# Issuing a memory-bound kernel's first load ahead of the barrier that opens the program

## The chip, the cores and the metric

The kernel runs on one core of one Trainium2 chip. The time is microseconds of device time; most executions of a kernel agree within about 0.1%. Each execution also lists its span, the time from the program's own first instruction to its last; the span is 1.8 us shorter than the time in nearly every execution. Because the effect in question is near 0.2%, most comparisons below were timed in five rounds, with the kernel before timed on the same chip in the same rounds.

The names: SyncE issues loads, TensorE (PE in the profile) multiplies, VectorE (DVE) and ScalarE (ACT) work on rows of elements, and GpSimd (POOL) fills small tiles. A semaphore is a counter that one engine raises and another waits for. A large load is cut into packets, which the core's 16 DMA engines move.

## The reference, cut to what matters

One decode step for one token: an attention block over a long cache, and an MLP with a mixer, both fed by one layer norm and added to the input.

```python
xn = layernorm(A_x)                                   # one row of 1024
q = (xn @ A_wq)                                       # 1024 x 4096: 32 heads of 128
scores = einsum(q, k_cache) * 128 ** -0.5             # 4 kv heads, 65536 keys, 128 wide
o = einsum(softmax(scores), v_cache)
out = x + o @ A_wo + mixer_mlp(xn, B_w1, B_w2, B_w3, B_w4)
```

Every weight and both caches are bf16 and are read exactly once. There are 170 MB of them, and one token's worth of arithmetic, so the work is mostly a read of memory.

## The kernel before

SyncE issues all the large loads, in one fixed order, into three buffers of 8 MB. A load is issued as soon as a buffer comes free. The first three entries (wq, w3, and w1 with w2) find empty buffers and wait for nothing.

```python
stream = ["wq", "w3", "w12"]
for u in range(NU):                       # NU = 8
    ...                                   # ("K", u), ("V", u); "wo" before the last V
stream.append("w4")

class Stream:
    def pump(self):
        while self.next < len(stream) and self.held < SLOTS:     # SLOTS = 3
            ...
            self.load(it)
    def done(self, it):                   # called when the last reader of a buffer is emitted
        self.tiles.pop(it)
        self.held -= 1
        self.pump()
    def load(self, it):
        t = big.tile([P, ROW], BF16, name="big")                 # 128 x 32768
        go = nc.sync.dma_start
        if it == "wq":
            go(out=t[:], in_=A_wq.rearrange("(p c) n -> p (c n)", c=DC))
        elif it == "w3":
            go(out=t[:, 0:DC * F], in_=B_w3.rearrange("(p c) f -> p (c f)", c=DC))
        ...

x_row = ogpool.tile([32, D], BF16, name="x_row", tag="og")
nc.vector.memset(x_row[:], 0.0)
nc.scalar.dma_start(out=x_row[0:1, :], in_=A_x[0, 0:1, :])       # x, on ScalarE's queue
st.pump()
```

The program opens with a barrier that is not in this source; the framework puts it there. Each engine announces itself (a drain that raises a semaphore), GpSimd collects the four announcements behind four small memsets of its own, and then releases everybody. Only then does SyncE branch to the body and issue the load of wq.

The program ends in order: the last piece of w4 lands, two matmuls add it to the output row, ScalarE casts the row, a small DMA writes it, and a closing barrier follows.

## Time and profile before

| What | Kernel before | Read from |
|---|---|---|
| time | 402.86 us median (402.81 to 403.03, 4 runs) | times |
| span of the profiled execution | 400.9 us | the page's head |
| data moved by the loads' queue | 169.87 MB, 98.4% of sixteen engines' span | the page's queue list |
| issue of the first load | 0.73 us | timeline of SyncE |
| first data packet | 1.73 us | packet records |
| last data packet ends | 396.86 us | packet records |
| from there to the end | 4.04 us | difference |

First the page's slice rows for the DMA engines: the span in 40 equal slices, the mean busy share of the 16 engines in tenths, and the GB/s that they moved. Below are the loads' queue and the bytes.

```profile
DMA  9989999999999999999999999999999999999895
GB/s 412 425 366 433 451 425 425 503 425 418 414 419 432 418 497 420 425 418 425 432 433 471 425 425 418 433 432 432 464 420 425 418 445 394 428 481 432 380 418 205
...
q1 hardware_dynamic: 4560, 169.87, 98.4%
```

There is no slice in which the engines rest, apart from the last few. From its first packet to its last the stream takes 395.13 us, so it runs at 430 GB/s. The Trainium skill's page "DMA: Bandwidth & Descriptors", section Specifications, gives a fabric ceiling of 435 GB/s. The median 64 KB packet takes 2.42 us. Nothing but fewer bytes or an earlier start can therefore take much off this kernel.

Second, the start. These are SyncE's DMA issues in the timeline (start in us, duration in us, what), and the line of SyncE's own waits for the opening barrier (total, times, longest).

```profile
0.73 0.37 SPq L128 DMA_DIRECT2D big<-in_A_wq_dram  x1
1.16 0.42 SPq L130 DMA_DIRECT2D big<-in_B_w_dram  x1
1.63 0.42 SPq L132 DMA_DIRECT2D big<-in_B_w_dram  x1
2.10 0.52 SPq L133 DMA_DIRECT2D big<-in_B_w_dram  x1
```

```profile
SPq L459 <- PEq L459: 0.7, 1, 0.7
```

SyncE waits 0.7 us at the barrier. In the trace's instruction records it announces itself at 0.00 us, as the first of all engines, and is released at 0.65 us. The view puts the wait down to TensorE's queue (PEq), but TensorE had announced itself by 0.32 us; GpSimd's drain, which ends at 0.49 us, is the last thing that the barrier waits for.

Third, the first pieces of the chain of work that ended last, in order of time (start, length, what), and its last load.

```profile
0.67 0.07 issue
0.73 22.05 DMA big<-in_A_wq_dram
22.83 5.89 PE psq L245 x62
28.73 41.32 DMA big<-in_A_k_cache_dram
...
379.92 17.40 DMA big<-in_B_w_dram
```

And what follows the last packet, from the timeline of ScalarE: the cast and the issue of the output write.

```profile
397.78 0.58 ACT L443 CAST out_t<-psB 64x512 bf16<-64x512 f32 x1 [29.53 <-PE psB L179]
398.39 0.58 ACTq L444 DMA_DIRECT2D out_dram<-out_t  x1
```

The chain reads as if the matmuls on wq (psq) set the time of the next load. They release a buffer at 28.73 us, but the load issued then lands 41.32 us later, and 8 MB need only 19.3 us of the stream (by the packet records, from the first packet of one cache load to the first of the next). The rest of the time it stands in the queue behind loads issued earlier: its own first packet starts at 48.4 us. The chain follows what released an issue; it does not show that the issue came long before its data could flow.

### The profile page before, as it was taken

The numbers are of one execution on the slowest core, as the hardware profiler recorded it, in microseconds if no ns is written. First come the engines' busy times: TensorE is split into PE (matmuls) and PEld (weight loads), VectorE is DVE, ScalarE is ACT, GpSimd is POOL, SyncE is SP. The second block draws the span as 40 slices with busy tenths as digits, with TensorE's granted clock in tenths as the row PEclk, the third lists the DMA queues.
The fourth block names the chain that finished last, engine by engine and source line by source line (L and its number), as shares of the span: only waits on it lengthen the run. The fifth ranks groups of instructions, "written<-read, shape, count | busy, mean of one in ns | idle before, by whom it ended". The sixth has DMA issues, their size and how long they took to land.

```text
span 400.9 us, 2563 instructions
## 1 busy us (share of the span) xinstructions
PE 230.4 (57%) x1348; PEld 44.2 (11%) x854; DVE 209.0 (52%) x154; ACT 27.3 (7%) x35; POOL 5.3 (1%) x28
## 2 busy tenths in 40 slices
PE   0470970591668246922965195629453936594985
PEld 0210000010200110010102010201020002000231
DVE  0511010974196549644953894269349931975040
ACT  1001010003000200020002000100100020002000
POOL 2000000000000000000000000000000000000000
PEclk9995795597679666968796799568866986697999
DMA  9989999999999999999999999999999999999895
GB/s 412 425 366 433 451 425 425 503 425 418 414 419 432 418 497 420 425 418 425 432 433 471 425 425 418 433 432 432 464 420 425 418 445 394 428 481 432 380 418 205
DMA packets 4575, 170.01 MB, mean 424 GB/s; under 512 B 467, under 2 KB 469, under 8 KB 982
## 3 DMA queue, kind: packets, MB, share of 16 engines
q1 hardware_dynamic: 4560, 169.87, 98.4%
q8 instruction: 8, 0.13, 0.1%
q14 instruction: 1, 0.01, 0.0%
q10 hardware_dynamic: 6, 0.00, 0.0%
HBM read 169.87 MB, written 0.00 MB: 424 GB/s over the span
## 4 chain that ended last, share of the span: by engine, by line
DMA 52%; DVE 26%; PE 16%; ACT 3%; another core or an unknown queue 2%; issue 1%; DVEq 0%; ACTq 0%
DMA big<-in_A_k_cache_dram 31%; DVE big L315 19%; DMA big<-in_A_v_cache_dram 10%; PE sc L320 8%; PE oacc L370 6%; DMA big<-in_A_wq_dram 6%; DMA big<-in_B_w_dram 4%; DVE p_sb L341 3%; DVE mx L325 3%; ACT p_sb L338 3%; PE psq L245 1%; PE pm_mx L327 0%; DVE m L329 0%; PE pm_mx L334 0%
## 5 line engine op out<-in xcount | busy, mean ns | idle before, releaser
L320 PE MATMUL sc<-big,qdiag 128*128 128x512 bf16 x512 | 127.7, 409 | 66.4 <-DVE big L315 66.4
L315 DVE STREAM_TRANSPOSE big<-big 128x4096 f32<-128x4096 f32 x32 | 139.4, 4413 | 50.5 <-DMA big<-in_A_k_cache_dram 50.4
L370 PE MATMUL oacc<-big,p_sb 128*32 128x512 bf16 x512 | 44.7, 521 | 34.5 <-DVE p_sb L341 34.5
L325 DVE TENSOR_REDUCE mx<-sc 128x1 f32<-128x2048 f32 x8 | 18.3, 2292 | 29.8 <-PE sc L320 29.8
L320 PEld LDWEIGHTS <-qdiag 128*128 128x128 bf16 x128 | 13.0, 102 | 176.6 <-issue 145.9
L338 ACT ACTIVATE p_sb<-sc,nball 128x2048 bf16<-128x2048 f32 x8 | 15.7, 1967 | 218.7 <-DVE nball L336 218.7
L341 DVE STREAM_TRANSPOSE p_sb<-p_sb 128x2048 bf16<-128x2048 bf16 x8 | 18.5, 2311 | 18.0 <-ACT p_sb L338 18.0
L370 PEld LDWEIGHTS <-p_sb 128*32 128x32 bf16 x512 | 16.6, 126 | 59.4 <-DVE p_sb L341 35.1
L245 PE MATMUL psh<-big,ln_rep_b 128*32 128x512 bf16 (+1 forms) x64 | 12.4, 941 | 8.0 <-DMA big<-in_B_w_dram 8.0
L409 PE MATMUL o_acc<-big,oT 128*1 128x512 bf16 x48 | 12.5, 428 | 2.4 <-ACT p_sb L338 2.4
L327 PE MATMUL pm_mx<-ident_f,mx 128*1 128x128 f32 x8 | 2.3, 283 | 19.1 <-DVE mx L325 19.1
L284 DVE STREAM_TRANSPOSE h_row<-h_row 128x896 bf16<-128x896 bf16 x1 | 1.1, 1111 | 21.1 <-ACT h_row L283 21.1
L379 DVE SCALAR_TENSOR_TENSOR og<-oacc,wb,og 128x512 f32<-128x512 f32 x4 | 3.0, 745 | 15.7 <-PE oacc L370 15.7
L179 PE MATMUL psB<-big,hT 128*1 128x512 bf16 x56 | 7.4, 378 | 1.8 <-DMA big<-in_B_w_dram 1.7
L193 PE MATMUL pm_ln<-ln_rowsum_a,ones_f 128*128 128x1 f32 x2 | 0.6, 347 | 13.3 <-DVE ln_rowsum_a L191 13.3
L415 DVE COPY o_rows<-o_acc 1x1024 f32<-1x1024 f32 x1 | 1.2, 1212 | 13.3 <-PE oacc L370 13.3
L184 DVE STREAM_TRANSPOSE x_t<-x_row 32x256 bf16<-32x256 bf16 x4 | 2.5, 616 | 8.9 <-DMA x_row<-in_A_x_dram 8.9
L269 POOL COPY qdiag<-qx 32x32 bf16<-32x32 bf16 x16 | 3.2, 203 | 279.9 <-PE sc L320 249.7
L391 PE MATMUL pm_e<-ol,sel8big 128*128 128x129 f32 x8 | 2.3, 370 | 8.2 <-DVE ol L390 8.2
L245 PE MATMUL psq<-big,ln_rep_a 128*32 128x512 bf16 x64 | 5.9, 547 | 1.3 <-DMA big<-in_A_wq_dram 1.3
L257 DVE CAST q_row<-psq 128x512 bf16<-128x512 f32 x1 | 0.7, 691 | 7.9 <-PE psq L245 7.9
L334 PE MATMUL pm_mx<-ident_f,rep 1*128 1x1 f32 x8 | 1.9, 241 | 5.0 <-DVE rep L331 5.0
(95 smaller groups left out, 72.6 us busy)
## 6 DMA issues: line engine op xcount, KB each, us to landing
big<-in_A_wo_dram SPq DMA_DIRECT2D x1, 8192.0 KB, 36.7
big<-in_B_w_dram SPq DMA_DIRECT2D x1, 7168.0 KB, 38.5
big<-in_B_w_dram SPq DMA_DIRECT2D x2, 2048.0 KB, 46.4
big<-in_B_w_dram SPq DMA_DIRECT2D x2, 1536.0 KB, 27.3
big<-in_B_w_dram SPq DMA_DIRECT2D x1, 1280.0 KB, 24.1
big<-in_B_w_dram SPq DMA_DIRECT2D x1, 1024.0 KB
big<-in_B_w_dram SPq DMA_DIRECT2D x1, 768.0 KB, 30.8
big<-in_B_w_dram SPq DMA_DIRECT2D x1, 512.0 KB, 31.5
```

Source lines behind the costliest of these rows:

```text
L179: nc.tensor.matmul(psB[32 * j:32 * j + lhsT.shape[1], :], lhsT=lhsT, rhs=rhs, start=start, stop=False, tile_position=(0, 32 * j), skip_gro ...
L184: nc.vector.transpose(out=x_t[32 * a:32 * a + 32].rearrange("p c j -> p (c j)"), in_=x_row[:, 256 * a:256 * (a + 1)].rearrange("p (i c) -> ...
L245: nc.tensor.matmul(acc[32 * q:32 * q + 32, i, 0:n], lhsT=rep[:, c, :], rhs=cols(c, i, q), start=(c == 0), stop=(c == DC - 1), tile_positio ...
L269: nc.gpsimd.tensor_copy(out=qdiag[at, LEAD:].rearrange("p (x c) -> p x c", x=4)[:, :, 32 * a:32 * a + 8], in_=qx[at, :, 8 * g:8 * g + 8])
L315: nc.vector.transpose(out=words, in_=words)
L320: nc.tensor.matmul(sc[:, e, :], lhsT=qdiag[:, c0:c0 + P], rhs=cols[:, s, e, :, b2, :, r], start=(s == 0 and b2 == 0 and r == 0), stop=(s = ...
L325: nc.vector.reduce_max(out=mx[:], in_=sc[:].rearrange("p e n -> p (e n)"), axis=AX.X)
L338: nc.scalar.activation(out=p_sb[:], in_=sc[:], func=ACTF.Exp, bias=nball[:, b:b + 1], scale=SCALE, accum_out=group["lall"][:, b:b + 1])
L341: nc.vector.transpose(out=flat, in_=flat)
L370: nc.tensor.matmul(oacc[32 * q:32 * (q + 1), :], lhsT=pT[:, e, 32 * t:32 * (t + 1)], rhs=vt[:, :, e, t, :], start=(e == 0 and t < 4), stop ...
L379: nc.vector.scalar_tensor_tensor(out=og[:], in0=oacc[:], scalar=wb[:, 1:2], in1=og[:], op0=ALU.mult, op1=ALU.add)
L409: nc.tensor.matmul(tail["rows"][0:1, h2, :], lhsT=oT[g][:, j:j + 1], rhs=wt[:, g, j, 512 * h2:512 * (h2 + 1)], start=(g == 0 and j == 0), ...
```

## The change

The first load needs nothing from the barrier: its buffer is untouched and its source is an input. A hook that runs when the program is finished moves that one instruction from the head of SyncE's body to the head of SyncE's entry block, ahead of its announcement at the barrier. No instruction is added or removed.

```diff
+def lead_with_the_first_load(nc):
+    blocks = [block for function in nc.m.functions for block in function.blocks]
+    entry = blocks[0]
+    body = next(b for b in blocks if any(i.opcode == "DMACopy" for i in b.instructions))
+    load = next(i for i in body.instructions if i.engine == mybir.EngineType.SP)
+    assert body is not entry and load.opcode == "DMACopy" and not load.sync_info.on_wait
+    body.instructions = [i for i in body.instructions if i is not load and i.name != load.name]
+    at = next(n for n, i in enumerate(entry.instructions) if i.engine == mybir.EngineType.SP)
+    entry.instructions = entry.instructions[:at] + [load] + entry.instructions[at:]
...
     nc.at_finalize(keep_loaded_weights)
+    nc.at_finalize(lead_with_the_first_load)
```

## The prediction

> What bounds the kernel now. The page's slice rows show the DMA engines at nine tenths or more almost throughout, and the queue list gives the loads' queue 98.4% of sixteen engines' span, for 169.87 MB. Its first data packet starts 1.73 us into the 400.9 us span and its last ends at 396.87 us (packet records): a stream of 395.1 us at 430 GB/s. The Trainium skill's page "DMA: Bandwidth & Descriptors", section Specifications, gives a fabric ceiling of 435 GB/s; the trace agrees: sixteen 64 KB packets at 2.42 us each are 434 GB/s. Idle engine time inside the stream sums to only 1.5 us, half of it in the last slices. So the time is the start, 395.1 us of stream, about 4 us of tail (last matmuls, cast, output write, closing barrier) and about 2 us outside the span (402.85 against 400.9).
>
> What the change does. In the timeline of the first microseconds, SyncE reaches the opening barrier first, at 0.00 us, waits for the others (0.7 us in the queue's own waits), and issues the 8 MB load of wq at 0.735 us; the issue takes 0.37 us and the first packet follows its start by 1.0 us. The change puts this issue ahead of the barrier, at 0.00 to 0.05 us. Nothing is added or removed. SyncE then arrives at the barrier at about 0.42 us (estimate: 0.37 plus an instruction's gap). [...] The three weight loads behind wq should be issued at about 0.73, 1.2 and 1.7 us instead of 1.16, 1.63 and 2.10.
>
> How much is on the critical path. The loads form one stream that never runs dry, so its start moves all of it. wq's landing (22.8 us) moves to about 22.1. Its consumers are ready: the first layer norm's result is done at 16.3 us, although x arrives only at 10.2 us, behind wq's first packets. x may come one packet round (2.4 us) later; 6 us of slack cover it. Later loads are issued as buffers come free, which follows landings and moves with them, each some 15 us before its data flow. So nearly the full 0.7 us should reach the end: first packet near 1.0 us, last end near 396.15, span near 400.2 us, a gain of 0.17%.
>
> Predicted time: 402.15 us, range 401.8 to 402.7. Faster by over 2%: 0.005; within 2%: 0.99; slower by over 2%: 0.005.
>
> What would show the steps right: wq's issue near 0.0 us; the barrier still opening at 0.65 us; wq's landing, later load issues and the last weight piece all about 0.7 us earlier; the stream still 395.1 us long; an unchanged tail.
>
> What would make it wrong: a slower first issue, or SyncE's drain waiting for the load, would open the barrier later, though only the first load's start counts; DMA rings not ready that early would leave nothing; a SyncE that starts later than now would hide the gain; a different interleaving of packets could move the stream by some tenths either way.

## The result, and the profile after

The changed kernel takes 402.10 us (402.02 to 402.14, 4 runs) against 402.86 us, and its output is correct. The ratio is 0.9982, with a 95% interval of 0.9968 to 0.9996. The gain of 0.76 us is small, but no execution of the one kernel overlaps with one of the other. Ratios here and below are not quite the ratio of the medians quoted.

The lines of the changed kernel that answer to those above (line numbers are 12 higher, since the hook was added): slices and queue, SyncE's issues, its wait for the barrier, the chain, and what follows the last packet.

```profile
DMA  9998999999999999999999999999999999999895
GB/s 419 419 453 371 435 471 458 426 419 419 421 426 465 452 426 414 426 426 432 445 460 426 419 426 419 447 439 452 426 421 426 432 445 385 432 481 426 385 417 201
...
q1 hardware_dynamic: 4560, 169.87, 98.6%
```

```profile
0.00 0.38 SPq L140 DMA_DIRECT2D big<-in_A_wq_dram  x1
0.78 0.33 SPq L142 DMA_DIRECT2D big<-in_B_w_dram  x1
1.16 0.42 SPq L144 DMA_DIRECT2D big<-in_B_w_dram  x1
1.64 0.52 SPq L145 DMA_DIRECT2D big<-in_B_w_dram  x1
```

```profile
SPq L471 <- PEq L471: 0.2, 1, 0.2
```

```profile
0.00 22.19 DMA big<-in_A_wq_dram
22.23 6.23 PE psq L257 x59
28.48 40.98 DMA big<-in_A_k_cache_dram
...
379.33 17.39 DMA big<-in_B_w_dram
```

```profile
397.19 0.58 ACT L455 CAST out_t<-psB 64x512 bf16<-64x512 f32 x1 [29.56 <-PE psB L191]
397.80 0.59 ACTq L456 DMA_DIRECT2D out_dram<-out_t  x1
```

The load of wq starts at 0.00 us, and the wait at the barrier shrinks from 0.7 to 0.2 us because SyncE now arrives later. In this trace the last load, the cast and the output write come 0.59 us earlier, and the tail keeps its length. Taken apart by the packet records, the two profiled executions compare like this:

| Part | before, us | after, us | difference |
|---|---|---|---|
| span's start to first data packet | 1.729 | 1.007 | -0.722 |
| stream, first packet to last | 395.134 | 395.270 | +0.136 |
| last packet to end of span | 4.043 | 4.048 | +0.005 |
| span | 400.906 | 400.325 | -0.581 |

The spans differ by 0.58 us and the times by 0.76 us. That is no loss, only the choice of the execution: over the 27 timed executions of the kernel before in the three sets of rounds below, the span is 400.9 to 401.3 us, mostly 401.0 or 401.1, so the profiled one is among its fastest, and the medians of the spans (401.0 and 400.3 us) differ by 0.7 us like the times. The ten profiled executions that move the same bytes on the loads' queue have streams of 395.13 to 395.45 us, and the shortest of them is that of the kernel before. The stretch of 0.14 us is inside that spread.

### The profile page after: what moved, and what is told of

Same layout as the page of the kernel before. It is cut to its first block, busy times and chain, and to the rows that moved or that the text cites. A ratio compares the mean times of both kernels' runs of the same rounds, so it can differ in the third digit from the quotient of the medians. Undisturbed runs are those within 1.5% of the kernel's fastest.

```text
span 400.3 us, 2563 instructions
## 1 busy us (share of the span) xinstructions
PE 236.0 (59%) x1348; PEld 45.2 (11%) x854; DVE 208.9 (52%) x154; ACT 27.3 (7%) x35; POOL 5.3 (1%) x28
## 4 chain that ended last, share of the span: by engine, by line
DMA 51%; DVE 26%; PE 16%; ACT 3%; another core or an unknown queue 2%; issue 1%; DVEq 0%; ACTq 0%
DMA big<-in_A_k_cache_dram 31%; DVE big L327 19%; DMA big<-in_A_v_cache_dram 10%; PE sc L332 8%; PE oacc L382 6%; DMA big<-in_A_wq_dram 6%; DMA big<-in_B_w_dram 4%; DVE p_sb L353 3%; DVE mx L337 3%; ACT p_sb L350 3%; PE psq L257 2%; DVE m L341 0%; PE pm_mx L339 0%; PE pm_mx L346 0%
## 5 line engine op out<-in xcount | busy, mean ns | idle before, releaser
L332 PE MATMUL sc<-big,qdiag 128*128 128x512 bf16 x512 | 129.5, 414 | 62.7 <-DVE big L327 57.2
L382 PE MATMUL oacc<-big,p_sb 128*32 128x512 bf16 x512 | 46.9, 539 | 34.5 <-DVE p_sb L353 34.5
```

Source lines behind the costliest of these rows:

```text
L332: nc.tensor.matmul(sc[:, e, :], lhsT=qdiag[:, c0:c0 + P], rhs=cols[:, s, e, :, b2, :, r], start=(s == 0 and b2 == 0 and r == 0), stop=(s = ...
L382: nc.tensor.matmul(oacc[32 * q:32 * (q + 1), :], lhsT=pT[:, e, 32 * t:32 * (t + 1)], rhs=vt[:, :, e, t, :], start=(e == 0 and t < 4), stop ...
```

## The experiments

The theory is: the loads are one saturated stream, its length does not depend on when it starts, and the time moves one to one with the start of its first packet. Rivals: part of the gain comes from the second to fourth load, which are issued 0.4 us earlier too (A); part of it comes from, or is lost to, the early compute, which starts with the barrier's opening and with x (B); or something else, such as where the measurement begins, made the difference. The traces already speak against that last one: counted from the span's start, GpSimd's first memset stands at 0.24 us before and 0.23 us after, so the moved load did not shift the zero against the other engines, and 1.8 us lie outside the span with either kernel.

The kernels of one set of rounds share the runs of the kernel before. Differences are those of the medians.

| Run | first issue, us | first packet, us | time, us | before, us | difference | ratio (95%) |
|---|---|---|---|---|---|---|
| after_again | 0.00 | 0.98 | 402.10 | 402.82 | -0.72 | 0.9981 (0.9968 to 0.9993) |
| between | 0.00 | 1.00 | 402.11 | 402.82 | -0.71 | 0.9981 (0.9969 to 0.9994) |
| all_four | 0.00 | 0.99 | 402.06 | 402.82 | -0.76 | 0.9981 (0.9969 to 0.9994) |
| rest_late | 0.00 | 1.00 | 402.06 | 402.82 | -0.76 | 0.9982 (0.9968 to 0.9995) |
| wq_late | 0.74 | 1.75 | 402.90 | 402.78 | +0.12 | 1.0009 (0.9995 to 1.0022) |
| x_behind_wq | 0.00 | 1.00 | 402.33 | 402.78 | -0.45 | 0.9990 (0.9977 to 1.0002) |
| one_piece_less | 0.00 | 0.99 | 401.40 | 402.78 | -1.38 | 0.9967 (0.9955 to 0.9980) |
| split_tail | 0.00 | 1.01 | 402.25 | 402.78 | -0.53 | 0.9987 (0.9975 to 1.0000) |
| after_third | 0.00 | 0.99 | 402.14 | 402.90 | -0.76 | 0.9983 (0.9970 to 0.9996) |
| behind_arrival | 0.08 | 1.08 | 402.25 | 402.90 | -0.65 | 0.9985 (0.9973 to 0.9998) |
| all_late | 2.76 | 3.77 | 404.89 | 402.90 | +1.99 | 1.0050 (1.0037 to 1.0064) |

### after_again and after_third: the yardsticks

> The changed kernel, unaltered, timed in the same rounds as the three below. All theories: about 0.75 us under the kernel before (402.1 against 402.86), as in the first result. It is here to be the yardstick of this call.

> The changed kernel once more, as the yardstick of this call: 402.1 us, 0.72 us under the kernel before.

They came out at 0.72 and 0.76 us under the kernel before, as in the first result. The gain repeats in three sets of runs.

### all_late: the start of the stream moved the other way

```diff
 # the kernel before: the pump moved behind GpSimd's last opening memset,
 # and a two-element memset by GpSimd into each buffer ahead of its load
+                nc.gpsimd.memset(t[0:1, 0:2], 0.0)
                 go(out=t[:], in_=A_wq.rearrange("(p c) n -> p (c n)", c=DC))
 ...                                      # the same for w3, w1 and w2
-    st.pump()
 ...
     nc.gpsimd.memset(g_col[:], 0.0)
+    st.pump()
```

> The run called wq_late was meant to start the stream 2 us later, but the loads were reordered and another one led, so that the stream started as before. Here all four weight loads of the kernel before wait for GpSimd's opening memsets, so that none is issued before about 2.75 us (0.735 us before). Theory (start of the stream passes on one to one): 2.0 to 2.1 us slower than the kernel before, about 404.8 us. Rival (something else set the gain): less than half of that.

The issues in its timeline, and the head of its chain of work from there:

```profile
2.76 0.37 SPq L129 DMA_DIRECT2D big<-in_A_wq_dram  x1
3.19 0.42 SPq L132 DMA_DIRECT2D big<-in_B_w_dram  x1
```

```profile
2.76 22.03 DMA big<-in_A_wq_dram
24.83 5.92 PE psq L249 x64
30.77 41.31 DMA big<-in_A_k_cache_dram
```

The first issue came 2.02 us later than in the kernel before, the first packet 2.04 us later, and the time was 1.99 us longer. With the change itself (first packet 0.72 to 0.75 us earlier, time 0.72 to 0.76 us shorter) this gives two doses of opposite sign, both passed on at their full size. In this run x also arrives ahead of the stream, at 2.5 us instead of 9.8 us by its packet records, and that buys nothing. The rival that something else made the gain falls with this and with GpSimd's unmoved memset.

### wq_late: a dose that missed, and what it showed anyway

```diff
 # the kernel before, with the memset ahead of the load of wq alone
+                nc.gpsimd.memset(t[0:1, 0:2], 0.0)
                 go(out=t[:], in_=A_wq.rearrange("(p c) n -> p (c n)", c=DC))
-    st.pump()
 ...
     nc.gpsimd.memset(g_col[:], 0.0)
+    st.pump()
```

> The kernel before, with its first load made to wait for the last of GpSimd's opening memsets, so that it is issued at about 2.8 us instead of 0.735 us; a dose in the other direction. Theory (start of the stream passes on one to one): 2.0 to 2.1 us slower than the kernel before, about 404.9 us. Rival (the time is bound elsewhere and the 0.75 us came from something else, such as where the measured time begins): less than half of that.

The time did not move as expected, and SyncE's issues in the timeline say why:

```profile
0.74 0.37 SPq L131 DMA_DIRECT2D big<-in_B_w_dram  x1
2.75 0.33 SPq L129 DMA_DIRECT2D big<-in_A_wq_dram  x1
3.13 0.43 SPq L133 DMA_DIRECT2D big<-in_B_w_dram  x1
```

The framework reordered the loads: w3, which waits for nothing, took the lead at the old moment, and the stream started at 1.75 us as before. So this was not a dose of the start but an unplanned change of order. wq landed at 39.5 us instead of 22.8 us, its matmuls began 17 us later, and the first cache load was issued at 44.7 us instead of 28.7 us. The median stayed within 0.12 us of the kernel before, with an interval that includes no change. (One of the five executions took 403.90 us, 1 us more than the other four; it has no trace, and its cause stays open.) That is further evidence for the theory: which load leads, and when its reader runs, does not matter much; when the first byte flows does. It was also close to the limit: by the packet records, which show the loads served in the order of their issue, the first cache load was due to flow at 48.35 us, so its lead was 3.7 us where the changed kernel has 19.2 us. No run here makes a lead negative, so what a load that comes too late costs was not measured.

### all_four and rest_late: do the other loads' issues count?

```diff
 # all_four: the four loads that wait for nothing, all ahead of the barrier
-    load = next(i for i in body.instructions if i.engine == mybir.EngineType.SP)
+    loads = [i for i in body.instructions if i.engine == mybir.EngineType.SP][:4]
 ...
-    entry.instructions = entry.instructions[:at] + [load] + entry.instructions[at:]
+    entry.instructions = entry.instructions[:at] + loads + entry.instructions[at:]

 # rest_late: the changed kernel, with the memset trick on w3's buffer alone
 # (and the pump moved behind GpSimd's memsets, as in all_late)
+                nc.gpsimd.memset(t[0:1, 0:2], 0.0)
                 go(out=t[:, 0:DC * F], in_=B_w3.rearrange("(p c) f -> p (c f)", c=DC))
```

> All four weight loads are issued ahead of the barrier, so that it opens about 1.3 us later (three more issues of 0.33 to 0.52 us), and x's load and every engine's first work come that much later, while the second to fourth load are issued 0.4 us or more earlier. Theory (only the start of the first load counts): same time as the changed kernel within 0.15 us, first packet still at 1.0 us after the first issue. Rival A (the earlier issue of the three other loads gives part of the gain): faster than the changed kernel by some tenths. Rival B (the opening of the barrier, or x's arrival, is on the path): slower than the changed kernel by 0.5 to 1.3 us.

> As the changed kernel, but the second weight load (and so the third and fourth) waits for the last of GpSimd's opening memsets, at about 2.8 us instead of 0.78 us. Theory: the first load alone gives the queue about 20 us of work, so the time is that of the changed kernel within 0.15 us. Rival A (the other loads' issue is part of the gain): slower than the changed kernel by up to 2 us, or at least by the 0.4 us that they moved in the change.

The first two issues of all_four, then of rest_late:

```profile
0.00 0.37 SPq L141 DMA_DIRECT2D big<-in_A_wq_dram  x1
0.42 0.42 SPq L143 DMA_DIRECT2D big<-in_B_w_dram  x1
...
0.00 0.37 SPq L140 DMA_DIRECT2D big<-in_A_wq_dram  x1
2.79 0.33 SPq L143 DMA_DIRECT2D big<-in_B_w_dram  x1
```

In all_four the barrier opened at 2.26 us instead of 0.70 us by the instruction records, x's load was issued at 3.02 us instead of 1.46 us, and the second load at 0.42 us instead of 0.78 us. In rest_late the second load was issued at 2.79 us. Both have a median of 402.06 us, 0.04 us from the changed kernel of the same rounds (402.06 to 402.15 us), though with a wider spread (up to 402.41 and 402.30 us). The issue of the other loads does not count in either direction (rival A falls), and neither does a barrier that opens 1.56 us later (rival B falls for the barrier). The first load alone gives the queue 20 us of work (its first packet starts at 1.0 us, that of the second load at 21.0 us).

### x_behind_wq: is early compute on the path?

```diff
                 go(out=t[:], in_=A_wq.rearrange("(p c) n -> p (c n)", c=DC))
+                go(out=x_row[0:1, :], in_=A_x[0, 0:1, :])
 ...
-    nc.scalar.dma_start(out=x_row[0:1, :], in_=A_x[0, 0:1, :])
```

> The changed kernel, with x's load taken from ScalarE's queue and put on SyncE's, directly behind wq. x should land at about 22 us instead of 9.4 us, and the first products with wq should start at about 28.5 us instead of 22.2 us, so that the buffer of wq comes free and the first load of the cache is issued about 6 us later, at about 34 us; its data are due to flow from about 47 us. Theory (the loads run far enough ahead; x and all early compute are off the path): same time as the changed kernel within 0.2 us. Rival B (early compute is on the path): slower by up to 6 us.

From the timeline of this run, the first use of x and the issue of the first cache load:

```profile
21.70 2.50 DVE L196 STREAM_TRANSPOSE x_t<-x_row 32x256 bf16<-32x256 bf16 x4 [18.74 <-DMA x_row<-in_A_x_dram]
...
38.83 0.33 SPq L160 DMA_DIRECT2D big<-in_A_k_cache_dram  x1
```

x came 12.2 us later than in the changed kernel (9.45 us there), and the first cache load was issued 10.4 us later (28.48 us there). Yet the profiled span is 400.35 us against 400.33 us, the last packet ends at 396.30 us against 396.28 us, and the spans of four of the five executions are 400.3 us. So inside the program 10 us of delay vanish, as the theory says: the first cache load's lead over its first packet fell from 19.2 to 8.8 us and stayed positive. The time, however, was 402.33 us, 0.29 us worse against the kernel before than the yardsticks' mean of 0.72 and 0.76 us would have it, which is more than the 0.2 us allowed. In all five executions of this run 2.0 us lie outside the span instead of the usual 1.8 us. What those 0.2 us are was not found. In this run alone ScalarE's queue issues nothing until the output, but no run tests whether that is the reason.

### between and behind_arrival: announce first, then load

```diff
 # behind_arrival (between was meant to do the same with `at += 1`)
-    at = next(n for n, i in enumerate(entry.instructions) if i.engine == mybir.EngineType.SP)
-    entry.instructions = entry.instructions[:at] + [load] + entry.instructions[at:]
+    at = next(n for n, i in enumerate(entry.instructions) if i.engine == mybir.EngineType.SP and i.opcode == "Drain")
+    entry.instructions = entry.instructions[:at + 1] + [load] + entry.instructions[at + 1:]
```

> The first load is issued after SyncE has announced itself at the opening barrier and before it waits for the release, so the barrier no longer waits for the issue. Theory (the gain is the earlier start of one saturated stream, passed on one to one): the load is issued at 0.05 to 0.1 us instead of 0.00, the barrier opens at 0.65 instead of 0.70 us, and the time is that of the changed kernel plus 0.05 to 0.1 us. Rival (the later barrier of the changed kernel eats part of the gain, because the other engines' start is on the path): 0.05 us faster than the changed kernel.

> The run called between was meant to issue the first load after SyncE's arrival at the barrier, but its trace shows the load ahead of the arrival: the same program as the changed kernel. This one puts it after the arrival and before the wait. Theory (start of one saturated stream): load issued at 0.05 to 0.10 us instead of 0.00, barrier open at 0.65 instead of 0.70 us, time that of the changed kernel plus 0.05 to 0.10 us. Rival (the 0.05 us later barrier costs something): faster than the changed kernel by 0.05 us or more.

The trace of between still has the load ahead of the announcement, so it is the changed kernel a third time over, and it says nothing about the question (it was 0.01 us from its yardstick). In behind_arrival the load does come second:

```profile
0.08 0.36 SPq L140 DMA_DIRECT2D big<-in_A_wq_dram  x1
0.73 0.33 SPq L142 DMA_DIRECT2D big<-in_B_w_dram  x1
```

The barrier opens at 0.65 us again, and the first packet comes at 1.08 us, 0.10 us later than in its yardstick. The time is 0.11 us longer (402.12 to 402.36 against 402.10 to 402.27). The sign and the size are what the theory says, but the ranges overlap, so this alone proves little. It gives the rival no support: opening the barrier earlier gained nothing.

### one_piece_less: the price of bytes

```diff
-                for n in W4_PIECES:
+                for n in W4_PIECES[:-1]:
 ...
-    compute_w4(early, FC)
+    compute_w4(early, FC - 1)
```

> The changed kernel without the last 256 KB piece of w4 and without the two products that use it; its result is wrong on purpose. Theory (saturated stream): 256 KB at 434 GB/s are 0.60 us, so 0.6 us faster than the changed kernel (0.55 to 0.75). Rival (the end is set by compute, such as the last attention products and the projection): 0.2 us or less.

(Its output still passes the comparison with the reference, since only one of 28 slices of a small term is missing; it is not the reference's sum all the same.) Its gain over the kernel before is 1.38 us, 0.64 us more than the yardsticks' mean of 0.74 us. The estimate from the stream's rate was 0.60 us. The end is set by the stream too, and 0.72 us of earlier start is worth about 310 KB of loads (0.72 us at 430 GB/s, an estimate from these two numbers).

### split_tail: a try at beating both

The tail of 4.0 us behind the last packet is serial, and a cast of 0.58 us is in it, so half of it was given to VectorE, and half of the output write to SyncE.

```diff
-    nc.scalar.copy(out=out_t[:], in_=psB[0:64, :])
-    nc.scalar.dma_start(out=..., in_=...)
+    nc.scalar.copy(out=out_t[:, 0:256], in_=psB[0:64, 0:256])
+    nc.vector.tensor_copy(out=out_t[:, 256:512], in_=psB[0:64, 256:512])
+    for h, queue in enumerate((nc.scalar, nc.sync)):
+        queue.dma_start(out=..., in_=...)             # half h
```

> The changed kernel with its last cast halved between ScalarE and VectorE and the output written by two loads' queues, ScalarE's and SyncE's, each half a row. Nothing in the stream changes. Theory (after the last packet there is a serial tail of 4.0 us: matmul, cast 0.58, issue 0.58, write, barrier): 0.2 to 0.4 us faster than the changed kernel, all of it after the last landing. Rival (the end is set by the write and the barrier): no gain.

The last compute and DMA instructions of its timeline (the bracket holds the idle time before and what ended it):

```profile
397.40 0.37 ACT L455 CAST out_t<-psB 64x256 bf16<-64x256 f32 x1 [29.58 <-PE psB L191]
397.80 0.59 ACTq L459 DMA_DIRECT2D out_dram<-out_t  x1
397.80 0.42 DVE L456 CAST out_t<-psB 64x256 bf16<-64x256 f32 x1 [7.37 <-ACT out_t L455]
398.24 0.60 SPq L459 DMA_DIRECT2D out_dram<-out_t  x1
```

VectorE's half did not start with ScalarE's; it was made to wait for it, and ran from 397.80 us. Halving the cast also did not halve it (0.37 and 0.42 us against 0.58 us). The two halves in a row plus an issue of 0.60 us end later than one cast and one issue: by 0.21 us, counted from the last packet of the loads (2.33 against 2.11 us). But the whole tail of the profiled execution grew only from 4.05 to 4.11 us, so how the median came to be 0.1 to 0.2 us worse than the changed kernel's is not settled; in the profiled execution, the slowest of the five, the stream is 0.23 us longer as well. No gain was to be had this way. No version tried here beats the changed kernel.

## Why the prediction was right

- **What bounds the kernel.** Right. One stream at 430 GB/s; one_piece_less priced its bytes at 0.64 us for 256 KB (0.60 us expected), and the streams of the ten profiled executions with the same bytes lie within 0.31 us of each other. (The prediction's 434 GB/s for sixteen packets is 433 by its own 2.42 us.)
- **The load's issue at 0.00 to 0.05 us.** Right: 0.00 us, with the first packet at 1.007 us (near 1.0 us expected).
- **The barrier "as before, at 0.65 us, at most 0.1 us later".** Right: 0.70 us. A detail was off: the arrival was put at 0.42 us. The drain did start at 0.424 us, but it took 0.131 us where it had taken 0.007 us, so the arrival came at 0.555 us, later than GpSimd's own readiness, and SyncE became the barrier's last arrival. The prediction had named a drain that waits for the load as a risk. all_four showed that a barrier opened 1.56 us later still costs nothing.
- **The other three loads at 0.73, 1.2 and 1.7 us.** They came at 0.78, 1.16 and 1.64 us; all_four and rest_late showed that it does not matter.
- **Later loads about 0.7 us earlier, because they follow landings.** Only in part. wq landed 0.6 us earlier (22.19 against 22.79 us), but the first cache load was issued only 0.25 us earlier, since the matmuls between took 6.23 us instead of 5.89 us, and the last cache load was even issued 0.1 us later (338.78 against 338.68 us). The stream held because these loads are issued far ahead, not because each issue moved. The prediction's "some 15 us" is about the smallest lead: in the changed kernel, every load from the first cache load on is issued 13.5 us or more before its first packet.
- **x may come one packet round later.** It came 0.8 us earlier in the profile (first use at 9.45 us against 10.25 us). The claim that slack covers a delay holds far beyond what was claimed: 12 us of delay left the span unchanged. That is more than the 6 us of slack that the prediction counted; the rest was covered by the lead of the loads.
- **Nearly the full 0.7 us reaches the end.** Right, and shown with both signs: 0.72 to 0.76 us for a first packet that is 0.72 to 0.75 us earlier, 1.99 us for one that is 2.04 us later. The predicted 402.15 us lies 0.05 us from the measured 402.10 us. The predicted span of 400.2 us was 400.33 us in the profile, because the stream of this execution was 0.14 us longer, a term the prediction named as a risk; it is within the spread of executions.

What stays open: the 0.2 us outside the span of x_behind_wq, the time lost in split_tail, the one execution of wq_late at 403.90 us, and what makes one execution's stream 0.1 to 0.3 us longer than another's. That the median came within 0.05 us of the prediction is partly luck, since the streams of single executions differ by up to 0.31 us.

## What to carry to other kernels

Where one stream of loads is saturated from its first packet to its last, and buffers run far enough ahead, the time is the moment of the first packet plus the stream plus the tail; delays of everything else cost nothing here as long as each load was still issued before its turn in the queue (the smallest lead tried was 3.7 us). Hoist the one load that needs nothing from the opening barrier and leave the others where they are. Before a change at a program's start, check that the wait it removes stands before the first byte, and judge its worth against the spread of the executions: here 0.18%, visible only because executions agree within 0.1%.

## What the Trainium skill lacked or had wrong

- "DMA: Bandwidth & Descriptors", section Specifications, gives a first-byte latency of about 0.6 us for loads issued by SyncE without saying from where it counts. From the start of the issue to the first packet it was 0.98 to 1.01 us in every run; counted from the issue's end (0.376 us long in the changed kernel) it was 0.63 us, which would agree.
- The same section lists about 358 GB/s as the limit of HBM for one core, and the section "Where 436 GB/s comes from" says that this side binds for loads from HBM. Neither passage says there that this holds with both cores of a pair streaming; the page says so under its table of measured rates, which gives 425 GB/s for 16 MB by a core whose neighbour is idle. Here the one core that the program runs on drew 430 GB/s for 395 us, so for such a case the table is what to go by, and the two passages read alone mislead.
- "VectorE: DVE Perf Modes", section "The DRAIN you can't avoid", calls the drains of the runtime's preamble and postamble about 12 ns and constant on all engines. The drains of this opening barrier stand inside the program, so they may not be the ones meant, and no page gives their length: SyncE's took 7 ns by itself, but 116 to 131 ns directly behind a DMA issue, and GpSimd's 184 to 196 ns.
- No page gives the cost of an opening barrier inside the program (only the runtime's own barriers around it are priced) or says what may be moved ahead of it. Here it held the first load until 0.73 us, and a load with no waits could be moved ahead of it.
